# Row copies of all heads at once: folds with fixed places, and another order of the steps, in a Sinkhorn attention with a Fourier mixer behind it

## Chip, core and metric

One core of a Trainium2 chip runs the whole program: four batches of a block attention and, on its output, a Fourier token mixer with a two-layer network. The metric is the device time of one execution in microseconds; lower is better. The engines are named as in the profile: PE (TensorE, matmuls), DVE (VectorE), ACT (ScalarE), POOL (GpSimd) and SP (SyncE, which issues DMAs only).

## What is computed

Shapes: B = 4, H = 8, S = 768, D = 64, 8 blocks of 96 tokens; the model width is 512 and the hidden width 2048.

```python
P = sort_net                                   # [B, H, 8, 8]; five rounds of
P = exp(P - max(P)); P /= P.sum(-1) + 1e-9; P /= P.sum(-2) + 1e-9
k_sorted = einsum('bhij,bhjcd->bhicd', P, k_blocks)     # the same for v
attn = softmax(q_blocks @ k_sorted^T / 8)      # within each of the 8 blocks
x = (attn @ v_sorted), heads side by side      # [B, S, 512]
mixed = real(fft(fft(x, axis=1), axis=2))
u = x + mixed
out = u + relu(layernorm(u) @ w_ch1) @ w_ch2
```

## The kernel before

**Steps and their order.** The kernel is written as a list of steps, each with the engines it may run on, a nominal duration on each, and the buffers that it reads and writes (`Plan.step`, L215; `chain`, L244, ties a matmul group to its evacuations). `Plan.run` (L330) picks step by step the one that can start first by these nominal durations, by priority among those that can start at nearly the same time; its choice fixes both the engine and the place in that engine's queue. All engines then work through their queues in order and wait on semaphores where data are missing. A step's priority comes from its batch, the length of the chain of steps behind it, and a table of offsets by step name and batch, `LEAD` (L190, four numbers per name, in thousands of the planner's units), added at L263. A number in the table thus moves all steps of one name in one batch forward or back in all queues, and can put a step on another engine.

**Stages of a batch.** `mix` makes the block-mixing matrix (`make_kron`, L542), turns q, mixes k and v, and forms the mean of the sorted values over each block (`means`, L619). `a24` (L648, on DVE) leaves these means as 24 rows in partitions 96 to 119 of a buffer `a24`: 8 rows of the rounded means, 8 of what the rounding lost, and 8 of the rounded means again. The attention works on values with their block mean taken away; `values` (L815) writes its normalized result for one head to `xr` ([99, 8 blocks, 512] in f16, two of them for alternate batches).

**The sequence transform.** For each pair of heads (128 columns) `fold` (L839) adds block j and block j + 4 of `xr` for the even outputs and subtracts them for the odd ones (L847, DVE, 96x512), into a buffer `xs`, of which there are two for all heads and both parities. In batches 1 to 3 the even half is folded once more (L852, two DVE instructions of 96x256) into a buffer `x4`, also one of two. Then `dft_s` (L867) multiplies by cosines and sines: `psWo` (L878) for the odd half, `psWe` (L891 and L895 in batch 0, L901 later) for the even half. Its first matmul takes 120 partitions and not 96: partitions 96 to 119 of the folded buffer must hold the rows of means of these 128 columns, which bring the means back.

**The row copies.** `rows_of_means` (L856, step `a_row`, L861) brings them there: one copy for each fold, 24x128 into `xs` (L858) or 24x2x128 into `x4` (L860), 32 in all, on DVE or POOL as the planner chooses; in the program 9 are on DVE and 23 on POOL. A copy can be issued only when the buffer is given to this fold, so it sits close ahead of, or behind, the fold itself.

**After it.** `fold_d` (L910) folds the result over columns, `dft_d` (L923) does the transform over the width (`psF`), `residual` (L974, L977) fetches the attention output in the transform's order of rows, `add_res` (L997, L998, always on POOL) adds the two to `u`, `stats`, `root`, `normal` (L1040, L1043) and `transpose_u` (L1056 by DMA, L1066 on PE) form the normalized transposed rows `unT`, and `mlp` runs the two layers: 16 groups of four matmuls (L1094, with `w1sb`) with ReLU on ACT, then for each of three row tiles 16 matmuls (L1115, with `w2sb`), for each half of the rows. A result leaves through `outt` (L1123) and an indirect DMA issued by POOL (L1138). The layers of batch b run beside the attention of batch b + 1 and b + 2 as far as the planner finds room; those of the last batch run alone at the end.

**POOL's queue** holds loads of q, k and the two weights (L502, L1151, L1155; one-element copies at L416 make some of them wait for an earlier one to land), sums of v (L521 to L523), the additions to `u`, a few normalizations, the row copies, and the stores of the output.

## Time and profile before

| what | value |
|---|---|
| median of 3 runs | 318.05 us (315.84, 318.05, 321.76) |
| the profiled execution: its own time | 315.49 us |
| its span, first to last instruction | 313.7 us |
| granted TensorE clock, mean over the span | 0.977 |
| PE busy | 279.9 us (89%) |
| DVE busy | 211.0 us (67%) |
| ACT busy | 195.0 us (62%) |
| POOL busy | 154.2 us (49%) |

The span starts with the first instruction; what the execution's time has beyond it, 1.8 us, lies around the program. A row of the groups gives source line, engine, operation, output and inputs with their shapes, then the busy time and the mean of one in ns, then the idle time of the engine just before these instructions and who ended it. A row of the timeline gives start and length in us, and in brackets the idle time before and its releaser. In the table by stage PEclk is the clock granted to TensorE in that stage, 1.00 being full speed. PEld is the load of a matmul's stationary operand, which runs beside PE. SPq and POOLq are the queues' own instructions.

### The profile page before, as it was taken

The numbers are of one execution on the slowest core, as the hardware profiler recorded it, in microseconds if no ns is written. First come the engines' busy times: TensorE is split into PE (matmuls) and PEld (weight loads), VectorE is DVE, ScalarE is ACT, GpSimd is POOL, SyncE is SP. The second block draws the span as 40 slices with busy tenths as digits, with TensorE's granted clock in tenths as the row PEclk, the third lists the DMA queues.
The fourth block names the chain that finished last, engine by engine and source line by source line (L and its number), as shares of the span: only waits on it lengthen the run. The fifth ranks groups of instructions, "written<-read, shape, count | busy, mean of one in ns | idle before, by whom it ended". The sixth has DMA issues, their size and how long they took to land.

```text
span 313.7 us, 7232 instructions
## 1 busy us (share of the span) xinstructions
PE 279.9 (89%) x2627; PEld 167.1 (53%) x2627; DVE 211.0 (67%) x481; ACT 195.0 (62%) x470; POOL 154.2 (49%) x241
## 2 busy tenths in 40 slices
PE   8878699699987799989999699979997999999990
PEld 5656567456644455545655356536644655645540
DVE  5699888998996687985869679995364864010010
ACT  4559657888752589959758489756604863704500
POOL 4634869697516999373284318643021963112020
PEclk9999879999999999999999989999999999999997
DMA  7963899985898666999979514577332437224021
GB/s 206 176 163 86 215 173 168 187 224 112 124 169 158 239 173 131 186 193 214 180 134 203 144 30 132 134 196 185 69 78 84 149 90 221 80 69 136 0 100 35
DMA packets 54174, 45.07 MB, mean 144 GB/s; under 512 B 23362, under 2 KB 46146, under 8 KB 54138
## 3 DMA queue, kind: packets, MB, share of 16 engines
q1 hardware_dynamic: 39338, 28.04, 34.0%
q0 software_dynamic: 14800, 16.57, 31.1%
q8 instruction: 20, 0.33, 0.4%
q14 instruction: 16, 0.13, 0.1%
HBM read 34.69 MB, written 12.58 MB: 151 GB/s over the span
## 4 chain that ended last, share of the span: by engine, by line
PE 52%; DMA 17%; POOL 9%; DVE 9%; issue 4%; ACT 3%; SPq 2%; POOLq 0%; DVEq 0%; ACTq 0%
PE bank L1094 23%; PE bank L1115 16%; DMA w2sb<-in_moe_w_ch_dram 5%; DMA out_dram<-outt,idx_sb 4%; POOL u L997 2%; PE bank L878 2%; POOL u L998 2%; DMA eT<-es 2%; DMA hr<-in_v_dram 2%; DMA v<-in_v_dram 2%; DVE vo L676 2%; PE bank L823 2%; SPq L684 2%; PE bank L701 1%; PE bank L745 1%
## 5 line engine op out<-in xcount | busy, mean ns | idle before, releaser
L1094 PE MATMUL bank<-unT,w1sb 128*128 128x384 f16 x512 | 92.4, 328 | 0.1
L1115 PE MATMUL bank<-w2sb,hr 128*128 128x512 f16 x384 | 90.0, 379 | 1.2 <-DMA w2sb<-in_moe_w_ch_dram 1.2
L1100 ACT ACTIVATE hr<-bank 128x384 f16<-128x384 f32 x128 | 61.1, 494 | 31.0 <-PE bank L1094 29.9
L1094 PEld LDWEIGHTS <-w1sb 128*128 128x128 f16 x512 | 48.0, 98 | 31.1 <-issue 1.2
L1115 PEld LDWEIGHTS <-hr 128*128 128x128 f16 x384 | 36.0, 98 | 40.6 <-issue 1.7
L1138 POOL DMA_INDIRECT out_dram<-outt,idx_sb x23 | 23.2, 1010 | 67.8 <-DVE outt L1123 33.2
L1123 DVE SCALAR_TENSOR_TENSOR outt<-ur,bank 128x512 f32<-128x512 f32 x24 | 16.4, 685 | 40.2 <-PE bank L1115 40.2
L781 ACT ACTIVATE sm<-bank,mns 96x96 f32<-96x96 f32 x128 | 32.0, 354 | 3.8 <-DVE mns L786 3.6
L1015 DVE BATCH_NORM_STATS2 st<-u 96x6 f32<-96x512 f32 (+1 forms) x32 | 21.9, 684 | 8.6 <-POOL u L998 8.6
L475 ACT CAST W<-bank 128x384 f16<-128x384 f32 (+1 forms) x37 | 12.6, 385 | 18.0 <-PE bank L878 11.1
L830 DVE TENSOR_TENSOR xr<-bank,rz 96x512 f16<-96x512 f32 x32 | 22.0, 686 | 1.1
L475 ACT COPY u<-bank 96x512 f32<-96x512 f32 (+1 forms) x24 | 13.6, 585 | 11.9 <-PE bank L974 9.1
L878 PE MATMUL bank<-cso_sb,xs 120*128 120x384 f16 (+1 forms) x64 | 13.8, 338 | 6.7 <-POOL xs L858 6.7
L997 POOL TENSOR_TENSOR u<-u,P 96x257 f32<-96x257 f32 (+1 forms) x16 | 11.6, 726 | 12.4 <-DVE P L955 4.2
L786 DVE TENSOR_REDUCE mns<-bank 96x8 f32<-96x768 f32 x16 | 15.0, 944 | 3.4 <-ACT hr L1100 2.5
L676 DVE SCALAR_TENSOR_TENSOR vo<-a,bank 128x384 f16<-128x384 f16 x32 | 15.7, 545 | 1.8 <-PE bank L672 1.7
L752 DVE TENSOR_REDUCE mxs<-bank 96x8 f16<-96x768 f32 x16 | 14.7, 943 | 0.3 <-PE bank L745 0.3
L823 PEld LDWEIGHTS <-eT 97*128 97x128 f16 x256 | 12.1, 102 | 5.2 <-POOL eT L812 0.7
L768 ACT ACTIVATE sm<-bank 96x768 f32<-96x768 f32 x16 | 12.6, 800 | 3.3 <-DVE rz L829 1.1
L847 DVE TENSOR_TENSOR xs<-xr 96x512 f16<-96x512 f16 x32 | 13.8, 445 | 0.5 <-PE bank L878 0.2
L823 PE MATMUL bank<-vs,eT 97*128 97x65 f16 x256 | 13.1, 200 | 1.0 <-POOL eT L812 0.6
L829 DVE RECIPROCAL rz<-bank 96x8 f32<-96x8 f32 x32 | 6.2, 195 | 9.8 <-PE bank L823 9.8
(146 smaller groups left out, 489.8 us busy)
## 6 DMA issues: line engine op xcount, KB each, us to landing
u_dram<-u SPq DMA_DIRECT2D x32, 192.0 KB
ur<-u_dram SPq DMA_DIRECT2D x24, 256.0 KB
v<-in_v_dram SPq DMA_DIRECT2D x11, 384.0 KB
vs<-vo SPq DMA_DIRECT2D x48, 65.0 KB
k<-in_k_dram POOLq DMA_DIRECT2D x15, 192.0 KB, 5.1
q<-in_q_dram POOLq DMA_DIRECT2D x15, 192.0 KB, 4.9
w1sb<-in_moe_w_ch_dram POOLq DMA_DIRECT2D x4, 512.0 KB, 7.0
w2sb<-in_moe_w_ch_dram POOLq DMA_DIRECT2D x4, 512.0 KB, 6.7
```

The costliest lines, as they stand in the source:

```text
L475: nc.scalar.copy(dst, src)
L676: ("vo", b, {"V": 560}, lambda e: nc.vector.scalar_tensor_tensor(vo[h // 4][:, :, h % 4, 0:D], a16s[b % 2].rearrange("p (h d) -> p h d", d ...
L781: nc.scalar.activation(sm.t[:, hh, j], pair(pS, BLK)[:, hh, j], AF.Exp, bias=mn.t[:, 4 * hh + j:4 * hh + j + 1], scale=-1.0)
L823: nc.tensor.matmul(ps[:, i // 4, i % 4], et[:, wide(i)], vs[2 * (b % 2) + h // 4][:, i, (D + 1) * (h % 4):(D + 1) * (h % 4 + 1)])
L830: nc.vector.tensor_tensor(xr2[b % 2][0:BLK, :, D * h:D * (h + 1)].rearrange("p (t j) d -> p t j d", t=2), ps[:, :, :, 0:D], r[:, :, :, Non ...
L878: nc.tensor.matmul(ps, xs[b, hp, 1].t[r, j, :], cso[r, j, :], start=(j == 0), stop=(j == 3))
L997: eng.tensor_tensor(u.t[0:n, 0:LH], u.t[0:n, 0:LH], l[0:n, 0:LH], op=ALU.add)
L1015: nc.vector.bn_stats(st.t[0:n], us[b, i, m].t[0:n])
L1094: nc.tensor.matmul(ps, w1sb[:, mc, 128 * fc:128 * fc + 128], unT[b, gr].t[:, mc, :], start=(mc == 0), stop=(mc == 3))
L1100: nc.scalar.activation(dst, bank(pH, [128, 384]), AF.Relu)
L1115: nc.tensor.matmul(ps, hr[f4].t[:, fc % 4, 128 * t:128 * (t + 1)], w2sb[:, fc, :], start=(fc == 0), stop=(fc == 15))
L1138: step("store", b, {"G": 1050}, lambda e: nc.gpsimd.indirect_dma_start(out=out.rearrange("b s m -> (b s) m"), out_offset=bass.IndirectOffs ...
```

## The change

- `xs` and `x4` as one of two buffers each are gone for the results of the folds. The odd folds of all four head pairs have places of their own in one tile `xo`, the even ones in a tile `xe`, for all batches. `xs` stays, without the rows of means, as the intermediate of the twofold fold in batches 1 to 3.
- The rows of means of all heads are copied at once: per batch one copy of 24x512 into `xo` and one or two into `xe` (the second half of `xe` is read with rows of means from batch 1 on only). 11 copies stand for 32. They may run on ACT and DVE, in batches 0 and 1 on POOL, too; in the program 6 are on DVE, 4 on ACT and 1 on POOL.
- A transform now depends on the copy of its kind in its batch and on its own fold. A copy has to wait until all transforms of that kind of the batch before have read the old rows.
- The columns kept for `make_kron` are those of batches 1 to 3 only.
- The table `LEAD` has other names and numbers, so all queues are in another order, and some steps that can run on several engines are on another one.

```diff
-    LEAD = dict(P=(0, 3, 0, 0), Q=(0, 0, -15.2, 0), a24=(0, -4.4, 0, 0), add=(0, -32.1, 0, 0),
...
+    LEAD = dict(P=(60, 29.7, 0, 0), We=(-33.7, 0, 0, -15.4), a16=(0, 6.5, 0, 0), a_row=(0, 0, -59.9, 0),
...
-    ring("xs", 2, [128, 4, 128], F16)
-    ring("x4", 2, [128, 2, 2, 128], F16)
+    ring("xs", 2, [BLK, 4, 128], F16)
+    xo = const.tile([128, 4, 4, 128], F16, name="xo")
+    xe = const.tile([128, 4, 2, 2, 128], F16, name="xe")
...
+    def rows_of_means(b):
+        src = a24[b % 2][TAIL].rearrange("p (h m) -> p h m", m=128)
+        for key, dst in (("xe0", xe[TAIL, :, 0, 0]), ("xo", xo[TAIL, :, 0]), ("xe1", xe[TAIL, :, 1, 0])):
+            if b or key != "xe1":
+                step("a_row", b, {"A": 590, "V": 350, "G": 800} if b < 2 else {"A": 590, "V": 350},
+                     lambda e, dst=dst: copy(e, dst, src) if e != "G" else nc.gpsimd.tensor_copy(dst, src),
+                     r=[("a24", b % 2)], w=[(key, "a")])
...
-            nc.vector.tensor_tensor(
-                xs[b, hp, par].t[0:BLK], xr[0:BLK, 0:4, ms], xr[0:BLK, 4:8, ms],
-                op=ALU.subtract if par else ALU.add)
+            dst = (xo[0:BLK, hp] if par else xe[0:BLK, hp].rearrange("p y j m -> p (y j) m") if t is None else t.t)
+            nc.vector.tensor_tensor(dst, xr[0:BLK, 0:4, ms], xr[0:BLK, 4:8, ms],
+                                    op=ALU.subtract if par else ALU.add)
...
-        step("a_row", b, {"V": 190, "G": 400} if par == 0 and b else {"V": 125, "G": 270}, rows_of_means,
-             r=[("a24", b % 2)], w=[(into, 0)])
...
-            plan.chain(("psWo", b, {"T": 650}, f, [(xs[b, hp, 1], 0), (xs[b, hp, 1], 1), "cso"], [pW]),
+            plan.chain(("psWo", b, {"T": 650}, f, [("xo", "a"), ("xo", hp), "cso"], [pW]),
...
-    pcs = const.tile([128, B * H, NB], F32, name="pcs")
+    pcs = const.tile([128, (B - 1) * H, NB], F32, name="pcs")
...
+        rows_of_means(b)
         for h in range(H):
```

The order of the instructions at three places follows. Line numbers of the changed kernel are 3 lower from the fold on; its store of the output is L1135, its additions L994 and L995, its loads of the first weights L1148.

POOL, from batch 2 into batch 3, before: stores of the output (L1138) and row copies alternate.

```order
204 L1138 DMA out_dram<-outt_145,idx_sb 3072x512
205 L858 COPY xs_108<-a_208 24x128
206 L860 COPY x_110<-a_208 24x2x128
207 L1138 DMA out_dram<-outt_146,idx_sb 3072x512
208 L858 COPY xs_108<-a_208 24x128
209 L860 COPY x_111<-a_208 24x2x128
210 L858 COPY xs_108<-a_208 24x128
211 L1138 DMA out_dram<-outt_145,idx_sb 3072x512
212 L1138 DMA out_dram<-outt_146,idx_sb 3072x512
213 L858 COPY xs_108<-a_208 24x128
214 L1138 DMA out_dram<-outt_145,idx_sb 3072x512
```

POOL at the same place of the changed program: there are stores and two normalizations (L1040), and no copies.

```order
188 L994 TENSOR_TENSOR u_126<-u_126,Q_122 96x257
189 L995 TENSOR_TENSOR u_126<-u_126,P_120 96x255
190 L1040 TENSOR_SCALAR un_140<-u_123,mv_128,rstd_134 96x512
191 L1135 DMA out_dram<-outt_146,idx_sb 3072x512
192 L1040 TENSOR_SCALAR un_139<-u_124,mv_128,rstd_134 96x512
193 L1135 DMA out_dram<-outt_146,idx_sb 3072x512
194 L1135 DMA out_dram<-outt_145,idx_sb 3072x512
195 L1135 DMA out_dram<-outt_146,idx_sb 3072x512
196 L1135 DMA out_dram<-outt_145,idx_sb 3072x512
```

The copies have left this queue; between the additions and the stores two normalizations have come in. The copies of batch 3 are now on DVE and ACT. On DVE of the changed program they stand here, behind the folds of the last head pair of batch 2 (rows 300 to 302):

```order
300 L855 TENSOR_TENSOR xs_109<-xr_198 96x512
301 L859 TENSOR_TENSOR xe<-xs_109 96x256 x2
302 L855 TENSOR_TENSOR xo<-xr_198 96x512
303 L787 TENSOR_REDUCE mns_101<-bank 96x8
304 L480 COPY xe<-a_208 24x4x128
305 L480 COPY W_114<-bank 128x2x4x48
306 L911 TENSOR_TENSOR W_115<-W_117,W_114 128x770
307 L912 TENSOR_TENSOR W_114<-W_117,W_114 128x770
308 L799 TENSOR_SCALAR es_103<-sm_97 96x4x96
309 L480 COPY xo<-a_208 24x4x128
310 L480 COPY ot_118<-bank 97x258
```

Rows 304 and 309 are the new copies; the third of that batch is on ACT.

POOL in batch 0, before: the loads of the first weights (L1151) stand between the sums of v, the fourth behind the first pair of additions.

```order
51 L1151 DMA w1sb<-in_moe_w_ch_dram 128x4x512
52 L521 TENSOR_TENSOR v_72<-v_72 128x2x192
53 L522 TENSOR_TENSOR vg_84<-v_72 128x128
54 L523 TENSOR_TENSOR vg_84<-vg_84,v_72 128x128
55 L1151 DMA w1sb<-in_moe_w_ch_dram 128x4x512
56 L521 TENSOR_TENSOR hr_68<-hr_68 128x2x192
57 L522 TENSOR_TENSOR vg_84<-hr_68 128x128
58 L523 TENSOR_TENSOR vg_84<-vg_84,hr_68 128x128
59 L997 TENSOR_TENSOR u_123<-u_123,P_119 97x257
60 L998 TENSOR_TENSOR u_123<-u_123,Q_121 97x255
61 L1151 DMA w1sb<-in_moe_w_ch_dram 128x4x512
```

POOL there in the changed program:

```order
61 L1148 DMA w1sb<-in_moe_w_ch_dram 128x4x512
62 L994 TENSOR_TENSOR u_125<-u_125,P_120 96x257
63 L995 TENSOR_TENSOR u_125<-u_125,Q_122 96x255
64 L994 TENSOR_TENSOR u_126<-u_126,Q_122 96x257
65 L995 TENSOR_TENSOR u_126<-u_126,P_120 96x255
66 L845 COPY xe<-a_208 24x4x128
67 L1148 DMA w1sb<-in_moe_w_ch_dram 128x4x512
68 L994 TENSOR_TENSOR u_123<-u_123,P_119 96x257
69 L995 TENSOR_TENSOR u_123<-u_123,Q_121 96x255
70 L994 TENSOR_TENSOR u_124<-u_124,Q_121 96x257
71 L995 TENSOR_TENSOR u_124<-u_124,P_119 96x255
72 L1148 DMA w1sb<-in_moe_w_ch_dram 128x4x512
```

The second, third and fourth load (rows 61, 67 and 72) stand behind two, four and six pairs of additions; the sums of v stand ahead of all of them.

More of the change, by code (lines that the diff above doesn't have):

```diff
@@ L549, in f @@
         def f(e):
-            s = pcs if src is None else src()
+            s = pcs[:, o.start - H:o.stop - H] if src is None else src()[:, o]
             plan.engines[e].tensor_tensor(
-                kron[b].t[:, hs], s[:, o, None, :].broadcast_to(shape),
+                kron[b].t[:, hs], s[:, :, None, :].broadcast_to(shape),
                 mask16[:, None, :, None].broadcast_to(shape), op=ALU.mult)
@@ L863, in fold @@
-        step("fold", b, {"V": 960 if par == 0 and b else 450}, f,
+            dst = (xo[0:BLK, hp] if par else xe[0:BLK, hp].rearrange("p y j m -> p (y j) m") if t is None else t.t)
+            nc.vector.tensor_tensor(dst, xr[0:BLK, 0:4, ms], xr[0:BLK, 4:8, ms],
+                                    op=ALU.subtract if par else ALU.add)
+            if t is not None:
+                for y, op in enumerate((ALU.add, ALU.subtract)):
+                    nc.vector.tensor_tensor(xe[0:BLK, hp, y], t.t[:, 0:2], t.t[:, 2:4], op=op)
@@ L864, in fold @@
+        step("fold", b, {"V": 960 if t is not None else 450}, f,
              r=[("x", b % 2, h, y) for h in (2 * hp, 2 * hp + 1) for y in range(2)],
-             w=[(into, 1)] + ([] if par or not b else [xs[b, hp, par]]))
+             w=[("xo" if par else "xe", hp)] + ([t] if t is not None else []))
     def dft_s(b, hp, par):
@@ L1230 @@
          r=[pC, (kron[0], 1)], w=["pca"])
[L1231 removed]
+    step("pcs", 0, {"A": 370, "V": 420}, lambda e: copy(e, pcs, pcol()[:, H:]), r=[pC, (kron[0], 1)], w=["pcs"])
     late += plan.todo[-2:]
```

40 lines of the change are left out of this document (14 added, 26 removed).

## Prediction

> **What bounds the kernel now.** I read the page's busy shares first, then the table by stage, then TensorE's list of waits, then the timeline around its longest waits. The page:
>
> ```profile
> span 313.7 us, 7232 instructions
> ...
> PE 279.9 (89%) x2627; PEld 167.1 (53%) x2627; DVE 211.0 (67%) x481; ACT 195.0 (62%) x470; POOL 154.2 (49%) x241
> ...
> PEclk9999879999999999999999989999999999999997
> ```
>
> TensorE (PE) is busy for 279.9 of 313.7 us; the change neither removes nor adds a matmul (5034 rows of TensorE in both programs), so what can move is the 33.8 us in which it stands, and the two dips of its clock, near 40 and near 180 us. By stage (busy time of PE first in each row, PEclk before the DMA share):
>
> ```profile
> core 0: us, PE busy (x) PEld busy (x) DVE busy (x) ACT busy (x) POOL busy (x), PEclk, DMA share, GB/s
> 20.00:40.00 20.00, 14.73 (x259) 10.85 (x258) 18.69 (x35) 14.81 (x22) 11.93 (x14) 0.91 0.55 130
> 160.00:180.00 20.00, 17.14 (x195) 9.59 (x194) 16.20 (x34) 12.21 (x39) 10.22 (x18) 1.00 0.84 172
> 200.00:220.00 20.00, 17.59 (x126) 9.66 (x124) 15.76 (x41) 13.28 (x38) 8.44 (x14) 1.00 0.69 177
> 220.00:240.00 20.00, 18.39 (x127) 9.97 (x126) 8.88 (x21) 7.38 (x17) 2.23 (x3) 1.00 0.33 82
> 280.00:300.00 20.00, 20.00 (x110) 10.67 (x109) 2.06 (x3) 7.75 (x16) 2.14 (x4) 1.00 0.23 77
> ```
>
> Until 40 us VectorE (DVE) has 18.69 us of 20 and PE waits for it. From 280 on PE has no gap at all, and what it does there (the last hidden layer) is what was put off. So a microsecond of PE idle taken out at 160 to 240 us reaches the end in full. Who makes PE wait (total us, times, longest):
>
> ```profile
> engine line waited for: us in total, times, longest us
> PE bank L878 <- POOL xs L858: 6.7, 3, 2.6
> PE bank L891 <- DVE xs L847: 2.4, 2, 1.4
> PE bank L615 <- DVE w2sb L563: 1.5, 1, 1.5
> PE bank L1066 <- DVE un L1043: 1.3, 1, 1.3
> PE bank L1115 <- DMA w2sb<-in_moe_w_ch_dram: 1.2, 1, 1.2
> ...
> PE bank L672 <- ACT u L475: 0.2, 1, 0.2
> ```
>
> The list has 26 rows and 24.3 us. Its longest is the one that the change touches: the odd half of the sequence transform (L878) waits three times for the row copy (L858) on GpSimd (POOL). One of the three, first POOL, then PE and DVE at the same time, then PE at the two others and the odd folds ahead of them:
>
> ```profile
> 207.85 1.00 POOL L1138 DMA_INDIRECT out_dram<-outt,idx_sb  x1 [1.05 <-DVE outt L1123]
> 211.68 0.29 POOL L858 COPY xs<-a 24x128 f16<-24x128 f16 x1 [2.83 <-DMA out_dram<-outt,idx_sb]
> ...
> 209.07 0.54 PE L901 MATMUL bank<-cse_sb,x 120*128 120x194 f16 x4
> 209.13 0.41 DVE L847 TENSOR_TENSOR xs<-xr 96x512 f16<-96x512 f16 x1
> 212.02 0.82 PE L878 MATMUL bank<-cso_sb,xs 120*128 120x384 f16 x4 [2.41 <-POOL xs L858]
> ...
> 174.97 0.41 DVE L847 TENSOR_TENSOR xs<-xr 96x512 f16<-96x512 f16 x1
> 178.79 0.82 PE L878 MATMUL bank<-cso_sb,xs 120*128 120x384 f16 x4 [2.63 <-POOL xs L858]
> ...
> 235.60 0.41 DVE L847 TENSOR_TENSOR xs<-xr 96x512 f16<-96x512 f16 x1
> 238.15 0.83 PE L878 MATMUL bank<-cso_sb,xs 120*128 120x384 f16 x4 [1.61 <-POOL xs L858]
> ```
>
> POOL issues a store at 207.85 and is done with it at 208.85, but its next instruction, a copy of 0.29 us, stands 2.83 us more until that store has landed. The other operand was there long before: the odd folds end at 175.38, 209.54 and 236.01, while PE had come to the point at 176.16, 209.61 and 236.54 (start less wait). So nothing else is late behind the copy; the next in line is DVE, in time by 0.07 us at the tightest.
>
> **The change, part by part.**
>
> *Removed waits.* 2.63 + 2.41 + 1.61 = 6.65 us. From batch 2 on the row copies go to DVE or ACT, three per batch, and the order puts them right behind the last transform of the batch before (DVE rows 304 and 309), a whole batch ahead of their use. I take all of 6.65; the bounds are 0 (another wait ends where they end) and 6.65.
>
> *The clock behind the first wait.* The same table in finer stages:
>
> ```profile
> 175.00:180.00 5.00, 2.37 (x17) 1.41 (x16) 2.81 (x6) 2.01 (x6) 1.31 (x2) 0.99 0.41 126
> 180.00:183.40 3.40, 3.40 (x24) 2.05 (x23) 2.79 (x5) 2.23 (x8) 0.25 (x1) 0.51 0.16 34
> 212.00:215.40 3.40, 3.38 (x28) 2.14 (x29) 0.93 (x3) 2.06 (x5) 1.29 (x2) 1.00 0.90 256
> 239.00:245.00 6.00, 6.00 (x47) 3.89 (x46) 3.58 (x7) 4.13 (x10) 2.84 (x4) 1.00 0.30 90
> ```
>
> Right after the wait of 2.63 us the granted clock is 0.51 for 3.40 us in which PE has no gap: 3.40 x 0.49 = 1.7 us lost. The waits of 2.41 and 1.61 us are followed by 1.00. If the dip is the work of the wait it goes with it, if not it stays: bounds 0 and 1.7. I take 1.7, since it starts 1.2 us behind the wait and the page shows no other dip after 60 us before the end. That it stays is a rival below. [...]
>
> *Copies.* 32 small ones become 11: POOL 23 to 1, DVE 9 to 6, ACT 0 to 4.
>
> ```profile
> L858 POOL COPY xs<-a 24x128 f16<-24x128 f16 x13 | 3.9, 296 | 14.5 <-DMA out_dram<-outt,idx_sb 11.9 <-PE bank L891 1.9 <-PE bank L878 0.4
> L860 POOL COPY x<-a 24x256 f16<-24x256 f16 x10 | 4.2, 438 | 13.2 <-PE bank L901 8.7 <-DVE a L648 4.4
> L858 DVE COPY xs<-a 24x128 f16<-24x128 f16 x7 | 3.0, 445 | 0.2
> L860 DVE COPY x<-a 24x256 f16<-24x256 f16 x2 | 0.4, 220 | 0.0
> L475 ACT COPY u<-bank 96x512 f32<-96x512 f32 (+1 forms) x24 | 13.6, 585 | 11.9 <-PE bank L974 9.1 <-PE bank L977 1.3 <-issue 1.2
> L858 DVE COPY xs<-a x7: 183/191/1544, 20.9 to 90.8; 24x128 f16<-24x128 f16 x7
> ```
>
> POOL gives up 3.9 + 4.2 = 8.1 us of work. A copy of 24x512 has no row. On DVE it lies between the 0.22 us of 24x256 and the 1.54 us that a smaller one once took; I take 0.3, being nearest in kind to the first: 6 x 0.3 = 1.8 against 3.4 us removed. On ACT four of at most 0.585 us, 2.3 us added to 195.0. None of it lies on the path, since the copies are issued far ahead of their use; DVE's 1.6 us less could help only where it is tight, and I count 0. If a DVE copy does take 1.54 us, an evacuation of the transform and the difference fold are queued behind it (rows 305 to 307), and PE waits for these: three batches at 1.54 - 0.22 = 1.3 us each give at most 4 us, a rival below. [...]
>
> *Places of their own.* The folds write the same sizes with the same number of instructions, and wait for transforms of the batch before, over 50 us earlier: 0. The smaller copy of the mixing columns: 0, one instruction.
>
> *The new order.* Everything else is reordered, too. On POOL the four loads of the first weights are now spread behind additions to the residual (six pairs ahead of the fourth, one before). What can be lost or won by the order is bounded by the other waits: 24.3 - 6.7, less 1.5 for L615 in the fixed head, is some 16 us. I see no row that says which way, and take 0, with half of it, 8 us, to either side as the ends.
>
> **Sum.** The profiled execution took 315.49 us (span 313.7); less 6.65 and 1.7 it would be 307.1. The median of the runs, 318.05, lies 2.6 above that execution; the same 8.3 us off the median gives **309.8 us**.
>
> **The rivals.** *The order wins as well.* DVE keeps PE waiting 2.4 us for folds at L891, where the new order puts two heads' matmuls in between, and 1.3 us at L1066, where additions no longer stand behind a weight load. With these, the 1.2 us at L1115 and another 1 us among the small ones, 6 us more: 304. For it speaks POOL's relief, against it that such waits come up wherever the order misjudges a duration.
>
> *The gain is given back.* New waits of the kind in the list (0.2 to 2.4 us each) open elsewhere, 4 us in all, or the DVE copies are held up in each batch (4 us), and the clock dips elsewhere (1.7): 309.8 + 4 + 1.7 = 315.5, within 2%. For it: the list has 25 such rows besides, and the changed order has been run by no trace that I have.
>
> *The dip stays.* The waits go, the half clock comes all the same, at another place: 318.05 - 6.65 = 311.4, just at the edge of 2%. For it: two waits of nearly the same length were followed by no dip; against it, PE would have no wait of such a length left in that half.
>
> *A weight load comes late: slower.* The rows:
>
> ```profile
> 65.42 0.71 POOL L998 TENSOR_TENSOR u<-u,P 96x255 f32<-96x255 f32 x1
> 65.05 0.81 PE L1094 MATMUL bank<-unT,w1sb 128*128 128x384 f16 x4
> ...
> 78.48 0.82 PE L1094 MATMUL bank<-unT,w1sb 128*128 128x384 f16 x4
> DMA to landing us min/median/max: 6.0/7.0/8.1
> ```
>
> The sixth pair of additions ends at 66.1 us at the old pace (65.42 + 0.71). Issue (0.8) and at most 8.1 us bring the fourth load in by 75.0. The first group that needs it is the 13th, which started at 78.48 (the first at 65.05). There are 3.5 us in hand. The additions have to come 3.5 us later before PE waits, 11.8 us before the gain is gone, and 18.2 us before it is slower by 2% (6.4 us). If the additions were 20 us late: 318.05 - 8.3 + 16.5 = 326. The DMA engines' near-full load there speaks for it, the length of the delay needed against it.
>
> *The change does nothing.* If the store's landing and not the copy held PE, the three waits would stay, and the time with them: 318. Against it speaks that PE's releaser is the copy and no DMA in all three.
>
> **Chances and range.** Forecast 0.36 (306 to 313; 0.33 of it under 311.7, the 2% mark, which is about what a measurement of this kernel can tell from no change), the order wins as well 0.18, the dip stays 0.12 (half of it under 311.7), given back 0.22, does nothing 0.04, a load late 0.08. Faster by over 2%: 0.33 + 0.18 + 0.06 = 0.57; within 2%: 0.03 + 0.06 + 0.22 + 0.04 = 0.35; slower: 0.08. The range reaches from 303, a little under the case in which the order wins as well, to 316.5, a little above the given-back case; the other two lie outside.
>
> **What would show it.** Right: no row of PE waiting for POOL or a copy in the list of waits; the odd transforms directly behind the even ones in batches 2 and 3; a clock of 1.00 from 100 us on; PE idle down by about 7 us and its busy time by 1.7. Wrong: a new row above 2 us in that list; PE waiting for `w1sb`; DVE copies of 24x512 above 1 us with PE waiting for the evacuation behind them. If the time falls with PE's other waits shrinking by more than 4 us, the order did it and not the copies.

## The result, and the profile after

| kernel | median, us | runs |
|---|---|---|
| before, on the same chip | 318.63 (313.97 to 367.33) | 20 |
| changed | 314.13 (310.92 to 320.08) | 20 |

The ratio of the undisturbed runs (those within 1.5% of the fastest of their kernel) is 0.9897, with a 95% interval of 0.9858 to 0.9936: about 3.3 us faster, and 4.5 by the medians of all runs, where 8.3 were forecast. The profiled execution of the changed kernel took 317.0 us (span 315.2), 2.9 us above its median, while that of the kernel before lay 3.1 below the 318.63 of the table; so these two traces are compared stage by stage and not by their ends.

The page of the changed kernel, busy times and clock:

```profile
span 315.2 us, 7188 instructions
...
PE 283.7 (90%) x2627; PEld 170.0 (54%) x2627; DVE 216.7 (69%) x471; ACT 197.0 (63%) x477; POOL 155.7 (49%) x223
...
PEclk9999659969999999999999999999999999999997
```

PE stands 31.5 us instead of 33.8. It is busy for 3.8 us more with the same 2627 matmuls, because they ran longer at half clock (20.5 us up to the last matmul, 10.2 in the trace of before): the dip near 180 us is gone, but the one near 40 us is deeper and there is a new one near 65. By stage, with the columns of the table shown before:

```profile
core 0: us, PE busy (x) PEld busy (x) DVE busy (x) ACT busy (x) POOL busy (x), PEclk, DMA share, GB/s
20.00:40.00 20.00, 14.45 (x240) 10.30 (x240) 14.99 (x29) 13.66 (x19) 7.16 (x11) 0.85 0.57 131
...
160.00:180.00 20.00, 19.83 (x227) 12.09 (x226) 17.34 (x40) 15.17 (x40) 8.34 (x15) 1.00 0.87 158
200.00:220.00 20.00, 18.86 (x140) 9.27 (x137) 19.24 (x43) 15.53 (x52) 14.27 (x14) 1.00 0.78 179
220.00:240.00 20.00, 20.00 (x141) 11.31 (x141) 9.79 (x24) 9.89 (x24) 1.95 (x2) 1.00 0.35 77
```

From 160 us on PE has become denser in each of the stages in which the waits were: 17.14 to 19.83, 17.59 to 18.86, 18.39 to 20.00. From 20 to 40 it has fewer matmuls (240, 259 before) at a lower clock (0.85, 0.91 before). PE's list of waits:

```profile
engine line waited for: us in total, times, longest us
PE bank L824 <- DMA vs<-vo: 3.3, 1, 3.3
PE bank L673 <- DVE ot L480: 2.0, 1, 2.0
PE bank L1091 <- DVE outt L1120: 1.9, 1, 1.9
PE bank L616 <- DVE w2sb L564: 1.5, 1, 1.5
PE bank L1063 <- ACT rstd L1022: 1.3, 1, 1.3
...
PE bank L934 <- ACT kz L478: 1.0, 1, 1.0
```

No row has a row copy any more; before, it led the list with 6.7 us. The new leader, 3.3 us, is the first product of the values (L824) in batch 0. Ahead of it, DVE first, then SP's queue, then PE:

```profile
19.15 3.53 DVE L753 TENSOR_REDUCE mxs<-bank 96x8 f16<-96x768 f32 x4
22.61 0.56 DVE L480 COPY qT<-bank 128x768 f16<-128x768 f16 x1
23.20 0.76 DVE L649 SCALAR_TENSOR_TENSOR a<-a,low_sb,bank 24x512 f16<-24x512 f16 x1
...
24.29 1.95 DVE L677 SCALAR_TENSOR_TENSOR vo<-a,bank 128x384 f16<-128x384 f16 x4
...
26.27 2.60 SPq L685 DMA_DIRECT2D vs<-vo  x4
28.91 0.61 SPq L495 DMA_DIRECT2D v<-in_v_dram  x1
29.57 1.20 SPq L685 DMA_DIRECT2D vs<-vo  x2
...
35.30 1.94 PE L824 MATMUL bank<-vs,eT 97*128 97x65 f16 x32 [3.34 <-DMA vs<-vo]
```

The same place in the kernel before:

```profile
20.10 0.76 DVE L648 SCALAR_TENSOR_TENSOR a<-a,low_sb,bank 24x512 f16<-24x512 f16 x1
...
21.22 3.81 DVE L676 SCALAR_TENSOR_TENSOR vo<-a,bank 128x384 f16<-128x384 f16 x8
...
23.20 5.72 SPq L684 DMA_DIRECT2D vs<-vo  x8
...
29.96 0.95 PE L823 MATMUL bank<-vs,eT 97*128 97x65 f16 x19 [0.35 <-DMA vs<-vo]
```

In the new order DVE does four maxima in a row and a copy of q ahead of the rounded means and the evacuations of the values (`vo`), which so start 3.1 us later. Their moves into `vs` start 3.1 us later as well, and a 384 KB load of the next batch's v stands ahead of the last two of six. The product starts 5.3 us later. Not all of this is the order's: in this execution DVE came 1.0 us late already to the first mixing matrix (`kron`, 14.51 us, 13.56 before), ahead of the maxima. Two kernels below that begin with the same steps (changed, filled; new order for 115 steps) come to it at 13.5 and 13.4 us and start the product at 34.3 and 34.5: 4.3 to 4.5 us later than before. From the first move to the first product it takes 9.0 us with the load in between and 6.8 before. The changed kernel is 12.0 us behind at the second half of batch 1's network (its first group starts at 184.6 us, 172.6 before) and 3.1 at the next half (215.8, 212.7): it lost time early and made most of it up between 172 and 212 us, where two of the three waits were.

### The profile page after: what moved, and what is told of

Same layout as the page of the kernel before. It is cut to its first block, busy times and chain, and to the rows that moved or that the text cites. A ratio compares the mean times of both kernels' runs of the same rounds, so it can differ in the third digit from the quotient of the medians.

```text
span 315.2 us, 7188 instructions
## 1 busy us (share of the span) xinstructions
PE 283.7 (90%) x2627; PEld 170.0 (54%) x2627; DVE 216.7 (69%) x471; ACT 197.0 (63%) x477; POOL 155.7 (49%) x223
## 4 chain that ended last, share of the span: by engine, by line
PE 50%; DMA 21%; DVE 10%; POOL 8%; issue 4%; SPq 3%; ACT 1%; POOLq 0%; DVEq 0%; ACTq 0%
PE bank L1091 20%; PE bank L1112 17%; DMA out_dram<-outt,idx_sb 5%; DMA w2sb<-in_moe_w_ch_dram 5%; DMA u_dram<-u 4%; PE bank L875 3%; DMA vs<-vo 2%; SPq L685 2%; DMA hr<-in_v_dram 2%; PE bank L824 2%; POOL u L995 2%; POOL u L994 2%; DMA q<-in_q_dram 2%; DVE mxs L753 1%; DVE vo L677 1%
## 5 line engine op out<-in xcount | busy, mean ns | idle before, releaser
L1091 PE MATMUL bank<-unT,w1sb 128*128 128x384 f16 x512 | 91.1, 326 | 1.9 <-DVE outt L1120 1.9
L1097 ACT ACTIVATE hr<-bank 128x384 f16<-128x384 f32 x128 | 60.0, 493 | 28.4 <-PE bank L1091 25.6
L1135 POOL DMA_INDIRECT out_dram<-outt,idx_sb x23 | 23.4, 1015 | 83.7 <-DVE outt L1120 58.3
L476 ACT COPY u<-bank 96x512 f32<-96x512 f32 (+1 forms) x20 | 11.5, 585 | 12.5 <-PE bank L971 8.2
L994 POOL TENSOR_TENSOR u<-u,P 96x257 f32<-96x257 f32 (+1 forms) x16 | 11.9, 744 | 14.7 <-DVE P L952 7.6
L522 POOL TENSOR_TENSOR v<-v 128x384 f32<-128x384 f32 x11 | 11.6, 1052 | 14.1 <-ACT v L476 8.6
L824 PE MATMUL bank<-vs,eT 97*128 97x65 f16 x256 | 13.4, 206 | 4.0 <-DMA vs<-vo 3.3
L824 PEld LDWEIGHTS <-eT 97*128 97x128 f16 x256 | 12.3, 106 | 7.5 <-DMA vs<-vo 3.5
L1040 POOL TENSOR_SCALAR un<-u,mv,rstd 96x512 f16<-96x512 f32 (+1 forms) x7 | 14.7, 2094 | 1.1 <-PE bank L746 0.7
L875 PE MATMUL bank<-cso_sb,xo 120*128 120x384 f16 (+1 forms) x64 | 14.2, 350 | 0.0
L1022 ACT ACTIVATE rstd<-mv,epst 96x2 f32<-96x2 f32 (+1 forms) x16 | 4.7, 295 | 14.6 <-DVE mv L1013 14.4
```

Source lines behind the costliest of these rows:

```text
L476: nc.scalar.copy(dst, src)
L824: nc.tensor.matmul(ps[:, i // 4, i % 4], et[:, wide(i)], vs[2 * (b % 2) + h // 4][:, i, (D + 1) * (h % 4):(D + 1) * (h % 4 + 1)])
L875: nc.tensor.matmul(ps, xo[r, hp, j], cso[r, j, :], start=(j == 0), stop=(j == 3))
L994: eng.tensor_tensor(u.t[0:n, 0:LH], u.t[0:n, 0:LH], l[0:n, 0:LH], op=ALU.add)
L1091: nc.tensor.matmul(ps, w1sb[:, mc, 128 * fc:128 * fc + 128], unT[b, gr].t[:, mc, :], start=(mc == 0), stop=(mc == 3))
L1097: nc.scalar.activation(dst, bank(pH, [128, 384]), AF.Relu)
```

## Experiments

In most of the kernels below the planner's choice is replaced by a recorded list (step, engine, buffer) of the kernel before or the changed one, so that nothing moves but what is named (where a recorded buffer is not free yet, the next free one is taken). `move` shifts one step in that list, and with it its instructions in all queues. Two places in each trace tell most: the start of the first product of the values, and that of the first group of the network (`w1sb`) in batch 0. Start and end of PE's rows in the profiled executions (one each: that of the kernel before lies 3.1 us below its median, that of the changed kernel 2.9 above, that with the v load moved 2.1 above, the others within 0.8):

| kernel | median, us | first product | first group | last matmul's end | from group to end |
|---|---|---|---|---|---|
| before | 318.63 | 30.0 | 65.1 | 305.7 | 240.6 |
| changed | 314.13 | 35.3 | 72.6 | 307.1 | 234.5 |
| change, old order | 308.81 | 29.9 | 64.8 | 299.7 | 234.9 |
| the same again | 307.48 | 29.8 | 64.4 | 297.4 | 233.0 |
| v load behind moves | 313.96 | 33.7 | 71.1 | 306.1 | 235.0 |
| v load and cast behind | 314.38 | 34.1 | 70.9 | 304.7 | 233.8 |
| changed, filled | 314.01 | 34.3 | 69.6 | 303.7 | 234.1 |
| new order for 115 steps | 312.17 | 34.5 | 68.5 | 301.8 | 233.3 |
| old order for 115 steps, mended | 312.83 | 30.0 | 69.1 | 302.0 | 232.9 |

**The change with the old order.** Steps at the places of the kernel before, copies right behind `a24`:

```diff
-plan.run()            # planner, new LEAD
+for step in order_of_before: ...   # a_row dropped there
+    after a24 of batch b: a_row(b) x2 or x3, on the engines of the changed kernel
```

> The change without its new order: fixed places xo and xe, one copy for all heads, 11 copies in place of 32, and every other step on the engine and at the place that it has in the kernel before; the copies stand right behind the rounded means (a24) of their batch. Theory A: 309 to 312 us, 2 to 5 us less than the changed kernel's 314.1, and the values' first product waits 0.4 us as before and not 3.3. Rival B: 314 us as the changed kernel, since the new order cost nothing and the copies alone bring no more than 4.5 us.

Measured 308.81 us, a ratio to before of 0.9721 (0.9645 to 0.9797); once more in a later round 307.48, 0.971 (0.9636 to 0.9783). Theory A, a little below its range. From the second trace, the top of PE's list:

```profile
PE bank L721 <- DMA k<-in_k_dram: 1.9, 2, 1.0
PE bank L1112 <- DMA w2sb<-in_moe_w_ch_dram: 1.8, 1, 1.8
PE bank L616 <- DVE w2sb L564: 1.5, 1, 1.5
```

No wait is longer than 1.8 us, and none is for a row copy. The change without its order is worth 10 to 11 us by the medians and 9 by the ratios, and the new order costs 5 to 7 of them (5.8 by the ratios). By the table it loses them before the first group (64.4 to 64.8 against 72.6, in an execution longer than its median); from there to the end both take 233 to 235 us, 5.7 to 7.6 less than before.

> The change with the old order once more, as the measure for the two others on the same chip and in the same rounds. Both theories: 308.8 us, within 1.5 us.

**The copies alone, in the kernel before.**

```diff
+for r in rows:
+    if r[0].name == "a_row" and r[0].b > 1:
+        r[1] = "V"
```

> The kernel before with its order held step by step; only the 14 row copies of batches 2 and 3 that were on POOL are put on DVE, each at the same place of the order. The same two buffers xs and x4, the same places, the same loads. Theory A (the forecast's sum for the removed waits is right, and the new order lost what is missing): the three waits of 6.65 us go and the half clock behind the first with them, so about 318.6 - 8 = 310.5 us (308 to 313), with no wait of PE on a row copy above 0.6 us. Rival B (gains of this kind are swallowed by the next wait, whatever the order): the three waits leave the list but others grow by 3 us or more, 314 to 318 us.

The three waits leave the list (its longest row on a fold is 0.6 us). The time is 315.26 us in 6 runs from 308.36 to 318.28, too spread for a ratio: inside Rival B's range by the median, while the lowest run lies in A's. Its trace is that of the longest run, and much of what makes it long lies ahead of the copies that were moved: a wait of 2.5 us for v at 8.8 us, one of 2.9 for `w2sb` ahead of 104.8, and 20.5 us at half clock between 35 and 74 us. From the first group to the end PE takes 238.0 us, 240.6 before. It is in favour of the direction and settles no size.

**The three stores behind the copies**, all else as before:

```diff
+move(("store", 1, 2), after=("a_row", 2, 7))
+move(("store", 1, 4), after=("a_row", 3, 1))
+move(("store", 2, 1), after=("a_row", 3, 7))
```

> The kernel before with its order held; on POOL three stores of the output stand behind the row copy that followed them, and not ahead of it; nothing else moves, the copies stay on POOL, in the same two buffers. Theory A (the copy stands until the store issued just ahead of it has landed): the three waits of PE on row copies (6.65 us) fall below 1 us each, and the time to 310 to 313 us. Rival E (the copies are late for another reason: the buffer, the engine): the waits stay at 1.6 to 2.7 us and the time at 318.5.

313.14 us, ratio 0.9853 (0.9793 to 0.9913): by the median just above the range of Theory A. None of the three waits is left where it was, and one of 2.4 us has come up at a later copy, behind the next store. POOL at that place:

```profile
212.53 1.04 POOL L1138 DMA_INDIRECT out_dram<-outt,idx_sb  x1 [0.35 <-DVE es L798]
216.13 0.29 POOL L858 COPY xs<-a 24x128 f16<-24x128 f16 x1 [2.56 <-DMA out_dram<-outt,idx_sb]
```

The copy stands 2.56 us until the store issued just ahead of it has landed, and PE's wait of 2.4 us is for this copy. The two copies that now have no fresh store ahead of them (at 177.47 and 205.93 us) do not stand for one; the third (233.11) still stands 1.9 us for an earlier store, but PE does not wait for it. That is the mechanism of the forecast, shown by moving nothing but the stores. The waiting is written in the program: POOL's queue in the kernel before has semaphore waits at the copies' own line, and in front of each of the three late copies there is one for the semaphore that the store raises when it has landed. In the run with the copies alone, no copy on DVE stands for a store.

```profile
L858 POOLq EVENT_SEMAPHORE  x9: 17/17/43, 40.4 to 237.7; - x9
```

**A load ahead of the moves, in both directions.** In the kernel before, the load of v is put ahead of the fifth move; in the changed one it is taken back behind the sixth:

```diff
+move(("load_v", 1, 0), before=("v_move", 0, 4))     # in the order of before
+move(("load_v", 1, 0), after=("v_move", 0, 5))      # in the order of the changed kernel
```

> The kernel before with its order held; one step is moved: the first load of batch 1's v stands ahead of the fifth move of the values in SP's queue, as in the changed kernel. Theory A: the values' first product (0.35 us of wait before) waits 1.2 to 2.5 us, and the time rises by as much, to 320 or 321 us; up to 324 if the half clock behind it gets longer. Rival C: 318.6 us as before, with a wait under 0.8 us.

320.38 us, ratio 1.0076 (1.0016 to 1.0136), with a wait of 2.1 us at the first product: Theory A. The price is 1.3 us by the medians (319.13 before on that chip) and 2.4 by the ratio. In its trace the moves also start 1.4 us later than before (24.6 us, behind a half clock from 18.4 us on), ahead of the load; from the first move to the first product it takes 8.6 us, 6.8 before, and these 1.8 us are the load's share.

> The changed kernel with its order held; one step is moved: the first load of batch 1's v stands behind the sixth move of the values (v_move) in SP's queue and not behind the fourth. Theory A: the wait of 3.34 us of the values' first product falls to between 1 and 2 us, and if the long half clock behind it (13.65 us) shortens to 6.83 us, another 3.4 us come back: 308.5 to 313 us against 314.1. Rival C (the moves are late because the evacuations of the values, vo, stand behind four maxima on DVE, and the load does not matter): the wait stays above 3 us and the time at 314.

The wait falls to 1.5 us as expected, and from the first move to the first product it takes 7.2 us instead of 9.0. The time does not fall: 313.96 us. What DVE does there now:

```profile
30.56 0.54 DVE L677 SCALAR_TENSOR_TENSOR vo<-a,bank 128x384 f16<-128x384 f16 x1
36.45 0.56 DVE L480 CAST v<-v 128x768 f16<-128x768 f32 x1 [5.34 <-DMA v<-in_v_dram]
```

The new order also has the cast of that load ahead of the first normalizations, so DVE stands for the load instead. With the cast and the sums moved too:

```diff
+move(("load_v", 1, 0), after=("v_move", 0, 5))
+move(("v_cast", 1, 0), after=("fold", 0, 1))
+move(("v_sum", 1, 0), after=("v_cast", 1, 0))
```

> The changed kernel with its order held and three steps moved: the first load of batch 1's v behind the sixth move of the values, as in the run with the load alone, and its cast on DVE and its sums on POOL behind the first two folds. Moving the load alone left the time at 314, and DVE stood 5.3 us in that cast, ahead of the normalizations. If that cast was what ate the gain: the wait of 3.1 us of PE on a normalization goes and the time is 311 to 312.5 us. Rival (the values themselves are late, and the place of the load and the cast only shifts the same wait): 313.5 to 314.5 us.

314.38 us: a miss, the rival holds. The long waits are gone (none above 1.4 us between 10 and 110 us), and yet the first product starts at 34.1 us. PE is late itself there, for it ran six stretches on end at half clock; the stretch ahead of them, the third and the last, each 3.41 us long (the clock stands behind POOL's share):

```profile
24.38:27.79 3.41, 2.33 (x32) 1.16 (x33) 3.41 (x7) 3.32 (x5) 2.24 (x3) 1.00 0.06 14
34.62:38.03 3.41, 3.41 (x47) 2.71 (x45) 2.45 (x6) 3.13 (x5) 0.00 (x0) 0.50 0.95 229
...
44.86:48.27 3.41, 3.41 (x33) 2.08 (x32) 2.99 (x7) 2.03 (x4) 2.98 (x5) 0.50 0.58 64
```

**Is the clock the loss?** The mean granted clock of the runs has a median of 0.959 with the changed kernel and 0.976 with the old order. So waits were filled with products of no use, 45 of them ahead of the first product of the values:

```diff
+for _ in range(n):      # n = 45, 10, 30, 18 ahead of psN, psWe, psV, psY
+    nc.tensor.matmul(free_columns_of_a_bank, junk[:, 0:128], junk[:, 0:128])
```

> The changed kernel, every step held, with 103 products of 128x128 by 128 columns of ones added in TensorE's queue (the output stays; their results are overwritten or not read): 45 ahead of the values' first product, 10 ahead of the second even transform of batch 0, 30 ahead of the second product of v in batch 1 and 18 ahead of the first transposes of the network's input, where TensorE waits 3.3, 0.8, 2.0 and 1.3 us. Each takes some 0.053 us, so they fill about 2.4, 0.5, 1.6 and 1.0 us of these waits. Theory J (the new order's loss is the clock: TensorE stands too long in a stretch of 3.41 us and then waits in nearly each stretch, which keeps the clock at half): the mean clock rises from 0.959 to 0.97 or more and the time falls from 314.1 to 309 to 311.5 us. Rival K (the half clock comes from the kind of work in that stage, not from the waits): clock and time stay, 0.96 and 314 us, or worse by what the added products delay.

The clock rises to 0.972, as Theory J has it, and the time stays at 314.01 us by the median, as Rival K has it. The ratio to before is 0.9824 (0.975 to 0.9898), against 0.9897 (0.9858 to 0.9936) for the changed kernel; the kernel before took 320.27 us in these rounds. So the filling gains nothing by the medians and 2.3 us by the ratios, whose intervals overlap. PE at the place that the 45 products fill:

```profile
30.88 2.69 PE L1492 MATMUL bank<-w2sb 128*128 128x128 f16 x45
34.26 1.15 PE L824 MATMUL bank<-vs,eT 97*128 97x65 f16 x32 [0.70 <-DMA vs<-vo]
```

With full clock up to 36.7 us the values still come at 34.3 us, 9.0 us after the first move, and in the changed kernel it was 9.0 us as well, with half clock from 34.0 us on. So up to the first product the clock is not the bound: PE waits for the values, or is slow until they come. From the first product to the first group it takes 35.4 us here and 37.3 in the changed kernel, so behind the first product the clock may have its part.

> The changed kernel with the load of v, its cast and its sums moved behind (314.4 us at a clock of 0.955; TensorE's idle time in its profile was 17.2 us, as little as with the old order), with 76 such products where TensorE waits for 0.3 to 0.5 us between 24 and 28 us (24 of them) and 1.0 to 1.4 us between 59 and 64 us (52). Theory J: clock 0.97 or more, 307 to 310 us. Rival K: 314 us.

314.51 us at a clock of 0.970, with a wait of 3.9 us at the first product again: the same answer for that stretch.

> The change with the old order (308.8 us, clock 0.976), with 46 such products ahead of the first and third product of the values, the first even transform of batch 0 and the first transposes. Theory J: clock 0.985, 305 to 307.5 us. Rival K: 308 to 309.5 us.

307.95 us at 0.980, ratio 0.9652 (0.9583 to 0.9722): between the two ranges, and not to be told from the old order without filling.

**Pieces of the orders.** The list of one order up to a step, then what is left in the sequence of the other:

```diff
+rows = first[:n] + [r for r in other if r not in first[:n]]     # n = 285 or 240, then 115
```

> The changed kernel's structure; the first 285 steps (up to the first group of the two-layer network of batch 0) stand in the order of the kernel before, all later ones in the new order. Theory A1 (the new order loses in its first 70 us: values late, v load and cast in the way, longer half clock): 308 to 310.5 us, as with the old order throughout (308.8). Rival D (the loss is spread over the later stages): 312 to 314 us, near the changed kernel's 314.1.

> The reverse: the first 240 steps (until batch 0's transform over the width is half done) in the new order, all later ones in the old order, with the changed structure. Theory A1: 313 to 315 us, with first products of the values at 33 us or later and the first group of the network at 70 us or later. Rival D: 309 to 311 us.

317.06 and 319.38 us, both worse than either order and than either theory: the cuts make waits of their own (3.5 us for a load of k in the first, 3.0 for `w2sb` in the second). Inconclusive. At 115 steps the two orders have done nearly the same:

> The changed structure; only the first 115 steps (batch 0 up to the first products of the values and the first fold) in the old order, all later ones in the new order. At this cut both orders have nearly the same steps behind them (4 differ), unlike at the cut of the run with 285. Theory F (waits and the copies gain the same with both orders, and the new order loses only clock, in these first steps): a mean clock of 0.970 or more and 308 to 311 us. Rival D (the clock is lost to the later order as well): a clock near 0.96 and 313 to 315 us.

> The reverse: the first 115 steps in the new order, all later ones in the old order. Theory F: a clock near 0.958 and 313 to 315 us. Rival D: a clock of 0.97 or more and 308 to 311 us.

313.54 us, which is Rival D's, and 312.17 us, between the two. Each half of the new order, with its cut, costs 4 to 5.5 us by itself against 308.1 as the middle of the two runs with the old order (5.4 and 5.7 by the ratios 0.9884 and 0.9893), and both together no more than 5 to 7. In the first of the two a load of k (2.8 us) and a fold (2.4 us) were late through the cut, so this was mended:

```diff
+move(("load_k16", 1, 0), before=("load_q16", 1, 0))
+move(("v_cast", 1, 0), after=("fold", 0, 1))
+move(("v_sum", 1, 0), after=("v_cast", 1, 0))
```

> The first 115 steps in the old order and the rest in the new one, as in the run that took 313.5 us, but without two waits that the cut itself made there (2.8 us for the load of k, 2.4 us of a fold behind a cast that waited for v): the load of k stands ahead of that of q, the cast and the sums of v behind the first two folds. Theory L: 309 to 311 us. Rival D (the new order loses behind these steps too): 312 to 314 us.

312.83 us: Rival D. The first product is at 30.0 us as with the old order, the first group at 69.1. PE's list has the load of k still, and further down three rows that the changed kernel has as well and the old order does not:

```profile
PE bank L721 <- DMA k<-in_k_dram: 2.6, 2, 2.3
PE bank L673 <- DVE ot L480: 2.1, 1, 2.1
...
PE bank L1063 <- ACT rstd L1022: 1.2, 1, 1.2
PE bank L934 <- ACT kz L478: 1.0, 1, 1.0
```

So a second loss lies between 55 and 66 us, where batch 0's transform over the width meets batch 1's first steps: 4.3 us in three waits, against 2.2 in three with the old order. That is 2.1 of the 4.6 us by which the first group is later than with the old order; the load of k, late through the cut, has 1.3 of the rest (2.3 us, 1.0 with the old order). So the price of this half alone is under what its run shows.

**Two maxima ahead.** The first loss as a dose of its own, put into the old order:

```diff
+move(("psS", 0, 3), before=("a_out", 0, 0))
+for k in (("max", 0, 2), ("max", 0, 3)):
+    move(k, before=("a24", 0, 0))
```

> The change with the old order, and one piece of the new order put into it: two of batch 0's maxima (0.87 us each on DVE, with the scores that they read) stand ahead of the rounded means and the evacuations of the values (vo), not behind them. Theory L (in the new order DVE comes to the evacuations too late, and everything in batch 0 behind them is late by as much): the first product of the values starts about 1.7 us later than with the old order (29.9 us), and the time rises from 308.8 to between 309.8 and 311.5 us. Rival M (PE has other work meanwhile and makes it up, since the maxima are done earlier): 308 to 309.3 us.

310.86 us, against 307.48 for the old order in the same rounds and 308.81 before: 2 to 3.4 us for 1.75 us of DVE's work at that place. Theory L. The ratios to before are 0.9796 (0.973 to 0.9861) and 0.971 (0.9636 to 0.9783); the intervals overlap, so the sign rests on the medians and on the moves of the values, which start at 25.1 us (23.2 in the kernel before). In its profiled execution, 3.6 us above the median, the first product starts at 34.0 us, later than the 1.7 us alone would have it; PE does not wait there but is late itself, with half clock from 23.2 us on.

**Stalls on purpose**, for the clock: in the change with the old order, PE is made to wait where it has no waits.

```diff
+for _ in range(n):                       # n = 2 to 5, at six groups of w1sb
+    nc.vector.tensor_copy(spare, ps)
+nc.vector.tensor_copy(c, c)              # c: the next group's weights
```

> The change with the old order, and six stalls of PE put on purpose into its last 70 us, where it has none: behind a group of the first layer DVE copies the result 2, 3, 4, 4, 3 or 2 times and touches the next weights (their values stay), some 1.3 to 2.4 us each by copies of about 0.5 us. Theory G (the clock is decided on a fixed grid of 3.41 us: a stretch with 2 us or more without matmuls is followed by half clock, one with less than 1.5 us is not): half clock behind the stalls above 2 us that lie in one stretch, none behind those that a boundary cuts in two or that are below 1.5 us. Rival H (length alone decides): the same answer for each length, wherever it lies.

> The same with 4, 5, 3, 4, 5 and 3 copies (1.8 to 2.9 us). Theory G: as before; of the stalls of 2.3 to 2.9 us about three in four are followed by half clock of 3.41 us, by where they lie on the grid. Rival H: all of them, or none.

The two kernels ran once each, in 319.35 and 330.76 us. The stalls took 0.85 to 3.08 us. Neither those of 0.85 and 1.31, nor five of 1.90 to 2.03, nor three of 2.49 us were followed by half clock; both of 3.08 were. Two pairs of stretches of the grid of the second kernel, with a stall of 2.49 and one of 3.08 us:

```profile
276.54:279.95 3.41, 1.86 (x12) 0.89 (x10) 1.44 (x3) 1.42 (x3) 0.00 (x0) 1.00 0.00 0
279.95:283.36 3.41, 2.47 (x15) 1.46 (x16) 0.85 (x3) 1.78 (x4) 0.00 (x0) 1.00 0.00 0
293.61:297.02 3.41, 1.07 (x7) 0.42 (x5) 2.75 (x5) 0.49 (x1) 0.89 (x2) 1.00 0.47 154
297.02:300.43 3.41, 2.67 (x9) 1.32 (x10) 0.65 (x3) 0.98 (x2) 0.45 (x1) 0.50 0.21 79
```

With 2.34 us of one stretch idle (3.41 less 1.07) half clock follows; with 1.55 (3.41 less 1.86) it does not, since a boundary cut the stall in two. The two stalls of 2.49 us of the first kernel left 1.89 us each in one stretch, and no half clock followed either. Of itself this would also fit a bound on the length between 2.49 and 3.08 us. Against that speaks the changed kernel's wait of 2.05 us at 62.3, which half clock did follow, with 2.09 us of its stretch idle. Theory G fits; its "three in four" does not, as none of the three stalls of 2.49 us was followed by half clock.

## Why the prediction was wrong, step by step

- **Removed waits, 6.65 us: right in mechanism, a little large in size.** The three waits are gone, in this kernel and wherever the copies left POOL, and the odd transform follows the even one at once:

```profile
176.90 0.50 PE L898 MATMUL bank<-cse_sb,xe 120*128 120x194 f16 x4
177.24 0.82 PE L875 MATMUL bank<-cso_sb,xo 120*128 120x384 f16 x4
```

  From the first group to the end PE takes 234.5 us instead of 240.6, and 233.0 and 234.9 with the old order: 5.7 to 7.6 us less, where this term and the next make 8.35. With that structure it is 231 to 236 in all kernels but the one cut at 285 steps (239.6) and the two with stalls.

- **The clock behind the first wait, 1.7 us: right in place.** In the changed kernel's trace the clock is 1.00 from 71.5 us to 310. With the stores alone moved, the half clock near 180 us is gone too; with the load moved in the order of before, where the waits stay, it comes at 178.8 us. Why one wait of three was followed by half clock, which the prediction left open, is the grid again. Stretches of the kernel before that hold the waits of 2.63, 2.41 (two stretches) and 1.61 us:

```profile
176.54:179.95 3.41, 1.16 (x8) 0.70 (x9) 1.30 (x3) 0.49 (x3) 0.30 (x2) 1.00 0.35 106
179.95:183.36 3.41, 3.41 (x24) 2.06 (x23) 2.79 (x5) 2.24 (x8) 0.21 (x1) 0.50 0.16 34
207.26:210.67 3.41, 2.35 (x14) 0.91 (x11) 3.31 (x11) 2.11 (x7) 1.00 (x1) 1.00 0.68 178
210.67:214.08 3.41, 2.06 (x16) 1.28 (x17) 0.84 (x2) 1.15 (x3) 1.61 (x3) 1.00 0.81 204
234.56:237.97 3.41, 1.98 (x12) 0.94 (x10) 1.38 (x5) 1.14 (x3) 1.07 (x2) 1.00 0.55 156
```

  2.25 us of one stretch were idle with the first wait; the second was cut into 1.06 and 1.35, and the third left 1.43. The clock as a whole went the other way in these two executions: 10.2 us were lost up to the last matmul in the changed trace and 5.1 in the one before (length of each half-clocked stretch times a half). The filled runs show that up to the first product this is not the bound; what it costs behind it, nothing by their medians and some 2 us by their ratios, stays open.

- **Copies, 0: right.** 24x512 takes 0.29 us on DVE (0.3 taken) and 0.61 on ACT (0.585 taken as the most):

```profile
L476 ACT COPY xo<-a 24x512 f16<-24x512 f16 x3 | 1.8, 614 | 2.5 <-DVE a L649 2.4
L480 DVE COPY xe<-a 24x512 f16<-24x512 f16 x5 | 1.4, 289 | 0.1
```

  Not one of the six on DVE took more than 0.29 us, so the worst case of 4 us did not come about.

- **Places of their own, 0: not shown apart.** The whole change with the old order gave 9 us by the ratios and 10 to 11 by the medians, a little more than the 8.3 of the sum.

- **The new order, taken as 0: this is the step that failed.** "I see no row that says which way" was true only of TensorE's list of waits of the kernel before. The order of the steps, which was at hand, said it: DVE's queue had four maxima and a copy of q ahead of the means and the evacuations, and SP's queue a load between the moves, while the row of DVE from 20 to 40 us (18.69 of 20) named the engine with the least room for anything put ahead there. The prediction looked at the queues where the copies were, and at POOL's weight loads. What it measured: 5 to 7 us, by the traces before the first group of the network. Put into the other order one by one, two maxima cost 2 to 3.4 us and the load 1.3 to 2.4. The 8 us that the prediction left to either side did cover this; the 0 in the middle did not.

- **The signs.** Right: no row for a row copy, the odd transforms directly behind the even ones, a clock of 1.00 from 100 us on. Not come: PE's idle time down by 7 us and its busy time by 1.7 (down 2.3 and up 3.8 in these executions). Of the signs of being wrong, the new row above 2 us came (3.3), PE waiting for `w1sb` and slow copies did not.

- **The rivals.** *Given back* (315.5) came nearest, and half of it happened: new waits opened elsewhere, 30 to 65 us into the program, with half clock beside them. It was the order that opened them; that DVE's copies would be held up, its other half, did not happen. *The order wins as well* is refuted by the old order being faster. *The dip stays*: not that dip (and of the "two waits of nearly the same length", 2.41 and 1.61 us, only the first was near). *A weight load comes late*: a load took 9.0 us in the median to land, 7.0 before, and yet PE has no wait for `w1sb`. *Does nothing*: refuted by the list.

What stays open is why the two losses of the new order do not add up, how much of them is the clock behind the first product, and whether its other stages win something. The new order with its maxima behind the evacuations was not tried. The best kernel that was run is the change with the old order, 307.5 to 308.8 us against 314.1 and 318.6; filling it adds nothing that can be told from it.

## What to carry to other kernels

When a change comes with a new order, price the order as a part of its own: go through the queue of the engine that is fullest in each stage, and ask what newly stands ahead of the steps that the bound engine waits for. Hold the order while the change is tried, for here the change was worth 9 to 11 us and its own order took more than half of it away. In the runs with the load and the cast moved, a wait that was taken out came back as the next one, or as half clock, while the values, which were really late, stayed where they were.

## What the runs showed of the hardware

In the traces the granted clock changed only on a grid of 3.41 us, which lay differently in each execution: up to the last matmul it was at half from 36.59 us on for 6.83 us and from 179.95 on for 3.41 in the kernel before, and from 33.98 on for 13.65 and from 64.70 on for 6.83 in the changed one. In the 20 traces (starts and lengths of all of PE's rows, from 5 us on up to the last matmul), a full-clocked stretch with 1.95 us or more without a matmul was followed by half clock in 21 of 21 cases, one with 1.4 to 1.95 us in 14 of 39, one with less in 11 of 1583, and all 11 lie between 24 and 62 us; what sets these 11 apart is not shown. It went back to full clock in 41 of 47 cases behind a half-clocked stretch with next to no idle time (under 0.05 us), and in 4 of 35 behind one with 0.2 us or more. Short waits alone stood beside a half clock that lasted: six stretches (27.79 to 48.27 us) in the run with load and cast behind, with no wait above 0.45 us in them, though the third of the six had no idle time at all and half clock followed all the same.

On POOL, a row copy stood until the indirect store issued just ahead of it had landed (2.83 us in the kernel before, 2.56 with the three stores moved), by a semaphore wait of the program; putting the stores behind the copies took all three of PE's waits away from their places and brought up one of 2.4 us behind the next store.
